# The output of a second feed-forward as seven block products in a phase of its own, on one Trainium2 core

## The chip, the cores and the metric

The kernel runs on one core of a Trainium2 chip. The metric is the device time of a run in microseconds (us), as the median of the runs; a profiled execution stands beside it, and all rows come from that. PE is TensorE (PEld its weight loads), DVE is VectorE, ACT is ScalarE, POOL is GpSimd, and SP is the engine whose queue issues nearly all DMAs.

## What is computed

Attention within chunks of 64 positions, then two feed-forward layers, all in float32:

```python
attn = softmax(q_c @ k_c.T / sqrt(64)); x = attn @ v_c      # x: 4608 x 512
h = x @ w_in; solu = h * softmax(h)                         # 1024 wide
x = ((solu - mean) / sqrt(var + 1e-6) * g_ln) @ w_out       # 4608 x 512
h = x @ w_in2; g = maximum(0.01 * h, h)                     # 2048 wide
out = g @ w_out2                                            # 4608 x 512
```

The weights arrive as float64 and are converted in the kernel by their bits. A float32 operand of a matmul is given as a high part, rounded to the matmul type float32r, and a low part, the rest. A product is then high x high, high x low and low x high: three matmuls.

## The kernel before

**The first phase** (L308 to L799) goes over 36 tiles t of 128 tokens: attention, first feed-forward with its softmax and normalisation, and its output y, which is stored by sixths (groups of 768 tokens) to `y_d` in DRAM. Beside this the weights are prepared in pieces. `load_next` loads a piece into one of four buffers, `take_magnitudes`, `convert_a` and `convert_b` convert it on ScalarE and VectorE, and `finish` calls the piece's `end`. `pieces` (L724) says how many an iteration takes: one, or two at t of 5 to 7. Of the 24 pieces, eight are of the first layer's w_out and sixteen of w_in2.

**The blocks.** The first product of the second layer, `h = y @ w_in2`, is computed by seven products of blocks in place of eight, in Winograd's form of Strassen's scheme. A piece of w_in2 for each half of the columns gives seven weight blocks (`want_in`, L172), split into high and low parts by ScalarE and GpSimd and stored to `wi_d` (L128). On the side of y, a group is cut into four blocks (a11, a21, a22, a12; two halves of 384 tokens, two halves of 512 features), four sums of them are made (`y_sum`), and seven operands are split (`y_split`): the high copy on ScalarE, the low part on GpSimd.

**The second phase** (L804 on) goes over 6 groups with 8 units j each. A unit is the seven products p1, p6, p2, p7, p5, p4, p3 in this order (`h2_product`), each of six matmuls of 384 columns, with weights that are streamed from `wi_d` by `w_load` into six buffers. The products use two PSUM banks in turn; p2 adds onto p1 in its bank, p7 onto p6, p4 onto that, p3 onto p5. What is read out between: p1 is copied by ScalarE, p6, p7, p5, p4 and p3 are added to kept results by VectorE (`with_ps`), and four of them end in `leaky`: Prelu on ScalarE, then high copy and low part (GpSimd) of an operand of the output product. So the bank of p4 must be read by VectorE before p1 of the next unit may write it (L825 to L828: the tags change sides with each unit).

The output product (`out_parts`) is a plain one: for each unit, twelve steps of six matmuls of 512 columns add to six PSUM banks, one per 128 tokens of the group. Two steps follow each of the first five products of the next unit, one each of the last two. Its weights w_out2 are converted once, in the first group, and stay in the core's memory (`wo_step`). Each engine runs its instructions in the order of the code, and DMAs on SP are issued in order; a DMA or instruction that waits holds up what is behind it on its queue.

## Time and profile before

| | |
|---|---|
| median of 3 runs | 1304.19 us (1303.96 to 1305.37) |
| the profiled execution | 1306.48 us, span 1304.7 us |
| granted TensorE clock, mean | 0.995 |
| busy share of the span: TensorE, weight loads, VectorE, ScalarE, GpSimd | 98%, 86%, 43%, 41%, 39% |
| DMA | 185.91 MB, mean 142 GB/s |

The span is the time from the first to the last instruction of the core; the execution's own time is 1.8 us longer. A busy time is a sum over instructions, so the engine with the largest share bounds the kernel only where it has no idle time between them. "Granted clock" is the share of 2.4 GHz that TensorE was given.

### The profile page before, as it was taken

How to read it: one execution, taken by the hardware profiler on the slowest of the kernel's cores; microseconds unless marked ns; L12 is line 12 of the kernel's file. 1: busy time of each engine (PE TensorE's matmuls, PEld its weight loads, DVE VectorE, ACT ScalarE, POOL GpSimd, SP SyncE). 2: the span in 40 equal slices, each digit the busy share in tenths (PEclk: the TensorE clock that was granted, in tenths of full speed). 3: DMA queues.
4: the chain of work that ended last, by engine and by line, in shares of the span. 5: the costliest groups of instructions: out<-in, count | busy, mean ns of one | idle time of the engine just before them, and what ended most of it. 6: DMA issues, size and time to landing. Idle time of an engine off the chain costs nothing.

```text
span 1304.7 us, 20560 instructions
## 1 busy us (share of the span) xinstructions
PE 1280.3 (98%) x7682; PEld 1118.3 (86%) x7682; DVE 556.6 (43%) x913; ACT 534.8 (41%) x1023; POOL 505.4 (39%) x601
## 2 busy tenths in 40 slices
PE   5999999999999999999999999999999999999998
PEld 4778888888888888889999999999999999999997
DVE  8678676767644443544641222122212221212112
ACT  6645445545443343344453334333333433343222
POOL 0356544555432222344572334234423532352222
PEclk9999999999999999999999999999999999999999
DMA  8435456554432214177654545544554455445342
GB/s 243 149 93 148 123 159 223 159 172 136 138 121 88 76 50 145 50 225 230 192 157 138 168 116 169 158 126 119 164 170 115 120 169 169 114 121 167 116 122 81
DMA packets 133778, 185.91 MB, mean 142 GB/s; under 512 B 47920, under 2 KB 69680, under 8 KB 132656
## 3 DMA queue, kind: packets, MB, share of 16 engines
q1 hardware_dynamic: 133232, 183.94, 47.0%
q8 instruction: 62, 1.02, 0.3%
q10 hardware_dynamic: 448, 0.66, 0.1%
q14 instruction: 36, 0.29, 0.1%
HBM read 151.00 MB, written 33.55 MB: 141 GB/s over the span
## 4 chain that ended last, share of the span: by engine, by line
PE 94%; DVE 2%; ACT 1%; DMA 1%; POOL 0%; issue 0%; SPq 0%; ACTq 0%
PE o_ps L877 30%; PE h_ps L834 27%; PE y_ps L505 15%; PE h_ps L423 14%; PE x_ps L395 3%; PE ln_ps L478 2%; PE s_ps L346 2%; PE pt_ps L379 1%; DMA raw<-in_w_in 1%; ACT es L577 0%; DMA qt<-in_q 0%; DVE wf L109 0%; DVE wf L105 0%; DVE wf L113 0%; DVE wf L103 0%
## 5 line engine op out<-in xcount | busy, mean ns | idle before, releaser
L877 PE MATMUL o_ps<-wo_s,g 128*128 128x512 f32 x1728 | 447.8, 391 | 0.8 <-POOL wo_s L303 0.8
L834 PE MATMUL h_ps<-yo,w_s 128*128 128x384 f32 x2016 | 406.9, 337 | 0.0
L834 PEld LDWEIGHTS h_ps<-yo,w_s 128*128 128x128 f32 x2016 | 362.8, 188 | 28.1
L816 POOL TENSOR_TENSOR g<-t,g 128x384 fp32r<-128x384 f32 x192 | 195.9, 1021 | 463.1 <-ACT g L815 389.9
L877 PEld LDWEIGHTS o_ps<-wo_s,g 128*128 128x128 f32 x1728 | 319.8, 188 | 43.0 <-POOL wo_s L303 1.3
L423 PE MATMUL h_ps<-wi,xs 128*128 128x512 f32 x864 | 211.5, 398 | 2.5 <-ACT xs L409 1.4
L505 PE MATMUL y_ps<-lnT,wo 128*128 128x512 f32 (+1 forms) x888 | 205.3, 387 | 1.0 <-POOL wo L120 0.8
L845 DVE TENSOR_TENSOR u<-h_ps,p 128x384 f32<-128x384 f32 x96 | 53.5, 557 | 335.1 <-PE h_ps L834 335.1
L423 PEld LDWEIGHTS h_ps<-wi,xs 128*128 128x128 f32 x864 | 160.2, 189 | 37.9 <-ACT xs L409 2.1
L505 PEld LDWEIGHTS y_ps<-lnT,wo 128*128 128x128 f32 x888 | 161.3, 188 | 34.7 <-DVE lnT L493 1.4
L813 ACT ACTIVATE t<-c 128x384 f32<-128x384 f32 x144 | 75.6, 525 | 264.6 <-DVE c L845 264.6
L369 POOL TENSOR_TENSOR es<-es,st 128x512 f32<-128x512 f32 x33 | 34.5, 1047 | 235.0 <-DVE st L368 211.0
L845 DVE TENSOR_TENSOR c<-h_ps,u 128x384 f32<-128x384 f32 x96 | 53.5, 557 | 129.4 <-PE h_ps L834 71.8
L815 ACT ACTIVATE g<-t 128x384 fp32r<-128x384 f32 x192 | 100.9, 526 | 6.1
L813 ACT ACTIVATE t<-h_ps 128x384 f32<-128x384 f32 x48 | 23.6, 491 | 186.1 <-PE h_ps L834 186.1
L445 DVE SCALAR_TENSOR_TENSOR us<-h_ps,us 128x1024 f32<-128x1024 f32 x36 | 44.1, 1225 | 61.3 <-ACT us L440 61.3
L440 ACT ACTIVATE us<-h_ps,z 128x1024 f32<-128x1024 f32 x36 | 40.1, 1115 | 54.7 <-DVE z L438 54.7
L513 ACT ACTIVATE ys<-y_ps 128x512 f32<-128x512 f32 x36 | 21.5, 596 | 99.8 <-PE y_ps L505 98.6
L493 DVE TENSOR_TENSOR lnT<-ln_ps,lnT 128x512 fp32r<-128x512 f32 x72 | 46.0, 681 | 33.7 <-ACT lnT L489 33.7
L413 DVE TENSOR_TENSOR xs<-x_ps,xs 128x512 fp32r<-128x512 f32 x36 | 24.8, 689 | 79.8 <-ACT xs L409 79.5
L845 DVE TENSOR_TENSOR c<-h_ps,p 128x384 f32<-128x384 f32 x48 | 26.8, 557 | 74.1 <-PE h_ps L834 74.1
L395 PEld LDWEIGHTS x_ps<-pt,vbd 128*64 128x64 f32 x1152 | 38.1, 142 | 15.7 <-issue 9.4
(87 smaller groups left out, 1153.5 us busy)
## 6 DMA issues: line engine op xcount, KB each, us to landing
w_s<-wi_d SPq DMA_DIRECT2D x336, 256.0 KB, 2.7
wi_d<-wi SPq DMA_DIRECT2D x8, 1792.0 KB, 7.6
raw<-in_w_out SPq DMA_DIRECT2D x24, 512.0 KB, 5.0
raw<-in_w_in SPq DMA_DIRECT2D x23, 512.0 KB, 4.4
vbd<-in_v SPq DMA_DIRECT2D x72, 128.0 KB, 3.6
a<-y_d SPq DMA_DIRECT2D x24, 384.0 KB, 5.7
qt<-in_q SPq DMA_DIRECT2D x35, 256.0 KB, 4.1
kbd<-in_k SPq DMA_DIRECT2D x70, 128.0 KB, 4.0
```

Source lines behind the costliest of these rows:

```text
L395: pe.matmul(ps[e * D : (e + 1) * D, i, c * D : (c + 1) * D], lhsT=vv[:, i, c, e], rhs=pp[:, i, c * D : (c + 1) * D], start=True, stop=True,)
L423: pe.matmul(h[:, n, :], lhsT=x[:, a, kk, :], rhs=w[:, b, kk % 2, n, :], start=(kk == 0 and a == 0 and b == 0), stop=(kk == KD - 1 and a == 1),
L440: act.activation(u, h, AF.Exp, bias=z[:, 0:1], accum_out=z[:, 1:2])
L445: dve.scalar_tensor_tensor(u, h, 1.0 / FF1, u, op0=ALU.mult, op1=ALU.mult, accum_out=z[:, 2:3])
L493: dve.tensor_tensor(dst[:, 1], ps, dst[:, 0].bitcast(F32), op=ALU.subtract)
L505: pe.matmul(ps[:, part], lhsT=w[:, a, kk % 4, m * P : (m + 1) * P], rhs=lnT[:, c, kk, pairs, :][:, part], start=(kk == 0 and a == 0 and c ...
L813: act.activation(t, src, AF.Prelu, alpha=0.01)
L815: act.activation(g[:, 0], t, AF.Copy)
L816: pool.tensor_tensor(g[:, 1], t, g[:, 0].bitcast(F32), op=ALU.subtract)
L834: pe.matmul(ps, lhsT=w[:, a, kk * P : (kk + 1) * P], rhs=y[:, c, kk, :], start=(first and kk == 0 and a == 0 and c == 0), stop=(kk == 1 an ...
L845: dve.tensor_tensor(o, ps, x, op=ALU.add)
L877: pe.matmul(ps, lhsT=x[:, a, i * P : (i + 1) * P], rhs=wos[j][:, h, c, :], start=(j == 0 and h == 0 and a == 0 and c == 0), stop=(j == QUA ...
```

## The change

The output product is computed by the same seven-product scheme. For a group, all eight units of the first product now run one after the other, and their results stay as four blocks (c11, c21, c22, c12), each in four tiles of two units (`leaky`, `blocks`). Sums of blocks (`block_sum`) are made on VectorE, three of them a pair of units, after products p6, p2 and p7 of units 2, 4 and 6; operands (`block_split`) by ScalarE and VectorE, the first four after p5 of units 1, 3, 5 and 7. Then come 28 slots of output (seven products of four pairs), each of six times a matmul of 512 columns (the high part against high and low weights, side by side) and one of 256 (the low part against the high weights), into two PSUM tiles of three banks. A slot's weights, 512 KB, are streamed from `wo_d` into six buffers (`wo_load`). Results are added on VectorE (`result`) and stored a product later (`out_store`).

w_out2's blocks are prepared in the first phase as those of w_in2 are (`want_out2`), so it has 40 pieces and sixteen stores; six more iterations take two pieces (`DOUBLE`), and the store of a block is issued at the start of an iteration. All low parts of operands in the second phase are on VectorE; nine tiles of w_in2 are loaded ahead instead of six. The last product of the last group goes token tile by token tile, so that its results leave early.

```diff
+PAIRS = QUADS // 2
+SLOTS = 7 * PAIRS
...
-WS = 6
+WS = 9
+WOS = 6
+RING = 11
 
 AHEAD = 5
+DOUBLE = (5, 6, 7, 10, 14, 18, 22, 26, 30)
...
+    wo_d = [dram.tile([P, 7, 2, 2, 2 * P], F32, name=f"wo_d{i}") for i in range(PAIRS)]
...
+    def want_blocks(srcs, dst):
...
-            stores.append((wi_d[j], w.bitcast(F32)))
-
+            stores.append((dst, w.bitcast(F32)))
+
+        for src in srcs:
+            queue.append((src, KD * P, end))
+
+    def want_in(j):
+        srcs = []
         for h in range(2):
             i, c = divmod((j + QUADS * h) * P, 512)
-            src = w_in2[i].rearrange("p (k n) -> p k n", k=KD)[:, :, c : c + P]
-            queue.append((src, KD * P, end))
+            srcs.append(w_in2[i].rearrange("p (k n) -> p k n", k=KD)[:, :, c : c + P])
+        want_blocks(srcs, wi_d[j])
+
+    def want_out2(j):
+        i, a = divmod(j, 4)
+        rows = w_out2.rearrange("(h i) p f -> i p h f", h=2)[i]
+        srcs = [rows[:, :, a * DM + c : a * DM + c + 2 * P] for c in (0, 2 * P)]
+        want_blocks(srcs, wo_d[j // 2][:, :, j % 2])
...
-    def y_load(g):
+    def y_load(g, n):
         if g < NG:
...
+            name, r, c = (("a11", 0, 0), ("a21", 1, 0), ("a22", 1, 1), ("a12", 0, 1))[n]
+            yr[name] = yp.tile([P, 2, TH], F32, tag=name, name=name)
+            sync.dma_start(
+                out=yr[name], in_=y_d[g][:, 2 * c : 2 * c + 2, r * TH : (r + 1) * TH]
+            )
...
-                "s2": ("s1", "a11", ALU.subtract, None),
                 "s3": ("a11", "a21", ALU.subtract, "a21"),
+                "s2": ("s1", "a11", ALU.subtract, "a11"),
...
+    def operand(x):
+
+        o = yp.tile([P, 2, 2, TH], F32R, tag="ring", bufs=RING, name="yo")
+        act.activation(o[:, 0], x, AF.Copy)
+        dve.tensor_tensor(o[:, 1], x, o[:, 0].bitcast(F32), op=ALU.subtract)
+        return o
+
     def y_split(g, k):
         if g < NG:
             x = yr[("a11", "s2", "a12", "s3", "s1", "a22", "s4")[k]]
-            o = yo[g, PRODUCTS[k]] = yp.tile([P, 2, 2, TH], F32R, tag="yo", bufs=9, name="yo")
-            act.activation(o[:, 0], x, AF.Copy)
-            for i in range(2):
-                eng = dve if g == 0 and i == 0 else pool
-                eng.tensor_tensor(o[:, 1, i], x[:, i], o[:, 0, i].bitcast(F32), op=ALU.subtract)
-
...
+    wo_tiles = []
+    wo_order = ((i, name) for _ in range(NG) for name in PRODUCTS for i in range(PAIRS))
+
+    def wo_load():
+        at = next(wo_order, None)
+        if at:
+            w = wb.tile([P, 2, 2, 2 * P], F32R, tag="wo", bufs=WOS, name="wo_s")
+            sync.dma_start(out=w.bitcast(F32), in_=wo_d[at[0]][:, w_place[at[1]]])
+            wo_tiles.append(w)
...
-                    store_next()
...
+            for j in range(QUADS):
+                want_out2(j)
...
+                    for n in range(4):
+                        y_load(0, n)
...
+                store_next()
...
-                pieces = 0 if t in (1, 4) or t >= T - 2 else 2 if AHEAD <= t < AHEAD + 3 else 1
+                pieces = 0 if t in (1, 4) or t >= T - 2 else 2 if t in DOUBLE else 1
...
+                    y_split(0, 0)
+                    for name in ("s1", "s3", "s2"):
+                        y_sum(0, name)
+                    y_split(0, 1)
+                    y_sum(0, "s4")
+                    for k in range(2, 7):
+                        y_split(0, k)
...
 
-            t = wb.tile([P, TH], F32, tag="t", name="t")
-            act.activation(t, src, AF.Prelu, alpha=0.01)
-            g = gts[n, block] = wb.tile([P, 2, TH], F32R, tag="g", bufs=8, name="g")
-            act.activation(g[:, 0], t, AF.Copy)
-            pool.tensor_tensor(g[:, 1], t, g[:, 0].bitcast(F32), op=ALU.subtract)
+            j = n % QUADS
+            if j % 2 == 0:
+                blocks[block, j // 2] = wb.tile(
+                    [P, 2, TH], F32, tag=f"{block}{j // 2}", name=f"{block}{j // 2}"
+                )
+            act.activation(blocks[block, j // 2][:, j % 2], src, AF.Prelu, alpha=0.01)
...
+        def block_sum(name, i):
+            x, y, op, to = {
+                "s1": ("c21", "c22", ALU.add, None),
+                "s3": ("c11", "c21", ALU.subtract, "c21"),
+                "s2": ("s1", "c11", ALU.subtract, "c11"),
+                "s4": ("c12", "s2", ALU.subtract, "c12"),
+            }[name]
+            if to:
+                blocks[name, i] = blocks[to, i]
+            else:
+                blocks[name, i] = wb.tile([P, 2, TH], F32, tag=f"{name}{i}", name=f"{name}{i}")
+            dve.tensor_tensor(blocks[name, i], blocks[x, i], blocks[y, i], op=op)
+
+        operands = {}
+
+        def block_split(s):
+            p, i = divmod(s, PAIRS)
+            x = blocks[("c11", "s2", "c12", "s3", "s1", "c22", "s4")[p], i]
+            operands[s] = operand(x)
+
+        sums = {}
+
+        def out_matmuls(p, i, kk, m, whole=True):
+            x, w = operands[p * PAIRS + i], wo_now[i]
+            ps = sums[p % 2][:, m]
+            first = p in (0, 1, 4) and i == 0 and kk == 0
+            last = i == PAIRS - 1 and kk == 1
+            c = slice(m * P, (m + 1) * P)
+            if whole:
+                pe.matmul(
+                    ps,
+                    lhsT=x[:, 0, kk, c],
+                    rhs=w[:, kk].rearrange("p a n -> p (a n)"),
+                    start=first,
+                    stop=False,
+                    skip_group_check=True,
+                )
+            else:
+                for a in range(2):
+                    pe.matmul(
+                        ps[:, : 2 * P],
+                        lhsT=x[:, 0, kk, c],
+                        rhs=w[:, kk, a],
+                        start=False,
+                        stop=False,
+                        skip_group_check=True,
+                    )
+            pe.matmul(
+                ps[:, : 2 * P],
+                lhsT=x[:, 1, kk, c],
+                rhs=w[:, kk, 0],
+                start=False,
+                stop=last,
+                skip_group_check=True,
+            )
+
+        wo_now, results = {}, {}
+
+        def out_product(s):
+            p, i = divmod(s, PAIRS)
+            if i == 0 and p in (0, 1, 4):
+                sums[p % 2] = pso.tile([P, 3, 512], F32, tag=f"o{p % 2}", name="o_ps")
+            wo_now[i] = wo_tiles.pop(0)
+            wo_load()
+            for kk in range(2):
+                for m in range(3):
+                    out_matmuls(p, i, kk, m)
+
+        def plus(o, p, a, x, m=slice(0, 3)):
+            dve.tensor_tensor(o[:, m], sums[p % 2][:, m, a * 2 * P : (a + 1) * 2 * P], x[:, m], op=ALU.add)
+
+        def result(p, m=slice(0, 3), halves=(1, 0)):
+
+            name = PRODUCTS[p]
+            if name in ("p1", "p6", "p2", "p7") and m.start == 0:
+                tag = {"p1": "p1", "p6": "u2", "p2": "c", "p7": "u3"}[name]
+                results[tag] = wb.tile([P, 3, 2 * P], F32, tag=f"o_{tag}", name=f"o_{tag}")
+            to, x = {
+                "p1": ("p1", None),
+                "p6": ("u2", "p1"),
+                "p2": ("c", None),
+                "p7": ("u3", "p1"),
+                "p5": ("u3", "u3"),
+                "p4": ("p1", "p1"),
+                "p3": ("u2", "u2"),
+            }[name]
+            o = results[to]
+            for a in halves:
+                if x is None:
+                    act.activation(o[:, m], sums[p % 2][:, m, 2 * P :], AF.Copy)
+                else:
+                    plus(o, p, a, results[x], m)
+                x = to
+
+        def out_store(g, p, eng=sync, m=slice(0, 3), rows=slice(0, P)):
+            at = {"p2": ("c", 0, 0), "p5": ("u3", 1, 1), "p4": ("p1", 1, 0), "p3": ("u2", 0, 1)}
+            if PRODUCTS[p] not in at:
+                return
+            o, r, c = at[PRODUCTS[p]]
+            first = g * TILES + 3 * r
+            dst = out[first : first + 3].rearrange("t p n -> p t n")
+            eng.dma_start(
+                out=dst[rows, m, c * 2 * P : (c + 1) * 2 * P], in_=results[o][rows, m]
+            )
+
+        for g in range(NG):
+            for j in range(QUADS):
+                if g == 0 and j < WOS:
+                    wo_load()
+                elif g and j == 1:
+                    out_store(g - 1, 6)
+                elif g and 2 <= j < 6:
+                    y_load(g + 1, j - 2)
+                for k in range(7):
+                    h2_product(g * QUADS + j, k)
+                    if g and j == 7 and k < 2:
+                        y_sum(g + 1, ("s1", "s3")[k])
+                    if j % 2 == 1 and k == 4:
+                        block_split(j // 2)
+                    if j % 2 == 0 and j and 1 <= k < 4:
+                        block_sum(("s1", "s3", "s2")[k - 1], j // 2 - 1)
+            for s in range(SLOTS):
+                p, i = divmod(s, PAIRS)
+                tail = g == NG - 1 and p == 6
+                if tail:
+                    wo_now[i] = wo_tiles.pop(0)
+                else:
+                    out_product(s)
+                if s < 2:
+                    for name in ("s1", "s3") if s == 0 else ("s2",):
+                        block_sum(name, PAIRS - 1)
+                if s + PAIRS < SLOTS:
+                    block_split(s + PAIRS)
+                if 9 <= s < 9 + PAIRS:
+                    block_sum("s4", s - 9)
+                for at, name in ((15, "s1"), (17, "s3")):
+                    if g == 0 and s == at:
+                        y_sum(g + 1, name)
+                if 19 <= s < 26:
+                    if s == 20:
+                        y_sum(g + 1, "s2")
+                    elif s == 23:
+                        y_sum(g + 1, "s4")
+                    y_split(g + 1, s - 19)
+                if g == 0 and s in (2, 5, 8, 11):
+                    y_load(1, s // 3)
+                if p and i == PAIRS - 1:
+                    out_store(g, p - 1)
+                if i == PAIRS - 1 and not tail:
+                    result(p)
+                    if g == NG - 1 and p == 4:
+                        plus(results["u2"], p, 1, results["u2"], slice(2, 3))
+        for m in range(3):
+            for i in range(PAIRS):
+                for kk in range(2):
+                    out_matmuls(6, i, kk, m, whole=m < 2)
+            if m:
+                result(6, slice(m - 1, m))
+                out_store(NG - 1, 6, sync, slice(m - 1, m))
+        result(6, slice(2, 3), (0,))
+        for eng, rows in ((sync, slice(0, 64)), (act, slice(64, P))):
+            out_store(NG - 1, 6, eng, slice(2, 3), rows)
```

## Rows read from the trace of the kernel before

**Rows 1.** The page, section 1: engine, busy us, share, instructions

```profile
PE 1280.3 (98%) x7682; PEld 1118.3 (86%) x7682; DVE 556.6 (43%) x913; ACT 534.8 (41%) x1023; POOL 505.4 (39%) x601
```

**Rows 2.** Windows, one group: us, busy of each engine, granted clock, DMA share, GB/s

```profile
676.40:801.00 124.60, 124.60 (x626) 112.99 (x625) 28.98 (x48) 42.94 (x82) 47.05 (x48) 1.00 0.49 144
```

**Rows 3.** The chain in order of time, two stretches: start us, us, what

```profile
528.76 0.70 DVE lnT L493
...
529.50 22.36 PE y_ps L505 x120
...
686.02 1.37 PE o_ps L877 x6
687.39 1.05 PE h_ps L834 x6
...
701.60 1.37 PE o_ps L877 x6
```

**Rows 4.** Timeline of the first unit: start us, us, engine, line, operation

```profile
551.71 8.53 PE L834 MATMUL h_ps<-yo,w_s 128*128 128x384 f32 x48
...
557.15 0.56 DVE L845 TENSOR_TENSOR c<-h_ps,u 128x384 f32<-128x384 f32 x1 [0.49 <-PE h_ps L834]
557.74 0.52 ACT L813 ACTIVATE t<-c 128x384 f32<-128x384 f32 x1 [1.13 <-DVE c L845]
```

**Rows 5.** Lines by form: busy us, mean ns of one, idle before and releaser

```profile
L813 ACT ACTIVATE t<-c 128x384 f32<-128x384 f32 x144 | 75.6, 525 | 264.6 <-DVE c L845 264.6
L845 DVE TENSOR_TENSOR c<-h_ps,u 128x384 f32<-128x384 f32 x96 | 53.5, 557 | 129.4 <-PE h_ps L834 71.8 <-ACT g L815 57.6
...
L255 ACT ACTIVATE yo<-a 128x768 fp32r<-128x768 f32 x24 | 19.9, 834 | 0.0
```

**Rows 6.** Timeline of VectorE at the third group's additions

```profile
747.18 1.41 DVE L249 TENSOR_TENSOR s<-a,a 128x768 f32<-128x768 f32 x1
750.87 0.56 DVE L845 TENSOR_TENSOR u<-h_ps,p 128x384 f32<-128x384 f32 x1 [2.28 <-PE h_ps L834]
751.34 0.95 DVE L249 TENSOR_TENSOR s<-s,a 128x768 f32<-128x768 f32 x1
```

**Rows 7.** Timeline of ScalarE in the first phase, two instructions in a row

```profile
168.71 0.67 ACT L96 ACTIVATE wf<-raw 128x512 f32<-128x512 f32 x1
169.28 0.59 ACT L385 ACTIVATE pt<-pt_ps 128x512 f32<-128x512 f32 x1
```

**Rows 8.** Windows of 3 us while the first weights are loaded

```profile
517.00:520.00 3.00, 3.00 (x15) 2.48 (x14) 1.73 (x2) 1.20 (x2) 1.52 (x3) 1.00 1.02 400
```

**Rows 9.** Windows, four iterations with pieces of weights and four without

```profile
151.52:209.30 57.78, 57.78 (x434) 47.83 (x433) 40.94 (x64) 28.53 (x50) 29.45 (x40) 1.00 0.54 174
382.46:440.08 57.62, 57.62 (x434) 47.90 (x433) 26.37 (x44) 22.93 (x40) 14.73 (x28) 1.00 0.25 74
```

**Rows 10.** Timeline of VectorE, low part of x, after one piece

```profile
176.35 0.69 DVE L413 TENSOR_TENSOR xs<-x_ps,xs 128x512 fp32r<-128x512 f32 x1 [2.26 <-ACT xs L409]
```

**Rows 11.** The page, section 5: the output's matmuls

```profile
L877 PE MATMUL o_ps<-wo_s,g 128*128 128x512 f32 x1728 | 447.8, 391 | 0.8 <-POOL wo_s L303 0.8
```

**Rows 12.** Timeline of the end

```profile
1291.74 9.00 PE L877 MATMUL o_ps<-wo_s,g 128*128 128x512 f32 x39
...
1301.42 0.42 DVE L888 COPY o<-o_ps 128x256 f32<-128x256 f32 x1 [1.31 <-ACT o L887]
```

**Rows 13.** Windows of 2 us in the first phase

```profile
72.00:74.00 2.00, 0.00 (x0) 0.00 (x0) 1.97 (x3) 1.88 (x4) 0.00 (x0) 1.00 0.94 314
74.00:76.00 2.00, 1.88 (x34) 1.88 (x36) 1.08 (x5) 1.93 (x5) 0.69 (x1) 0.53 0.62 205
76.00:78.00 2.00, 2.00 (x19) 1.70 (x18) 1.13 (x2) 1.35 (x3) 1.64 (x6) 0.61 0.18 42
```

**Rows 14.** Windows of 4 us near the start

```profile
12.00:16.00 4.00, 2.66 (x27) 2.21 (x25) 3.50 (x8) 3.40 (x19) 0.00 (x0) 1.00 1.11 308
```

**Rows 15.** Timeline of TensorE in that window

```profile
14.80 1.09 PE L346 MATMUL s_ps<-kbd,qt 128*64 128x128 f32 x16 [1.23 <-DMA kbd<-in_k]
```

More of the change, by code (lines that the diff above doesn't have):

```diff
@@ L170, in want_out1 @@
             queue.append((src, 4 * P, end))
-    def want_in(j):
+    def want_blocks(srcs, dst):
         kept = []
@@ L253, in y_split @@
             x = yr[("a11", "s2", "a12", "s3", "s1", "a22", "s4")[k]]
-            o = yo[g, PRODUCTS[k]] = yp.tile([P, 2, 2, TH], F32R, tag="yo", bufs=9, name="yo")
-            act.activation(o[:, 0], x, AF.Copy)
-            for i in range(2):
-                eng = dve if g == 0 and i == 0 else pool
-                eng.tensor_tensor(o[:, 1, i], x[:, i], o[:, 0, i].bitcast(F32), op=ALU.subtract)
-    Y_STEPS = [
-        ((4, 0), lambda g: y_split(g, 0)),
-        ((5, 0), lambda g: y_sum(g, "s1")),
-        ((5, 2), lambda g: y_sum(g, "s2")),
-        ((5, 4), lambda g: y_sum(g, "s3")),
-        ((6, 0), lambda g: y_split(g, 1)),
-        ((6, 3), lambda g: y_sum(g, "s4")),
-    ] + [((7, k - 1), lambda g, k=k: y_split(g, k)) for k in range(2, 7)]
+            yo[g, PRODUCTS[k]] = operand(x)
     w_tiles = []
@@ L700 @@
                     )
-                    y_load(0)
-                    stage = ctx.enter_context(
-                        tc.tile_pool(name="st2", bufs=2, side="right", reuse_waits="tile")
-                    )
-                    wf_bufs = 2
+                    for n in range(4):
+                        y_load(0, n)
                     for _ in range(WS):
                         w_load()
-                    for h in range(2):
-                        wo_load(0, h)
                 if t <= AHEAD:
@@ L899 @@
-        NQ = NG * QUADS
-        for n in range(NQ + 1):
-            g, j = divmod(n, QUADS)
-            parts = out_parts(n - 1) if n else iter(())
-            if n == NQ:
-                for _ in parts:
-                    pass
-                break
-            if j == 3:
-                y_load(g + 1)
-            for k in range(7):
-                h2_product(n, k)
-                for _ in range(2 if k < 5 else 1):
-                    next(parts, None)
-                if n == 0 and 2 <= k < 4:
-                    wo_load(1, k - 2)
-                if g == 0 and k < 6:
-                    for h in range(2):
-                        if (3 if j == 0 else 0) <= k - h < 5:
-                            wo_step(j, h, k - h)
-                for at, do in Y_STEPS:
-                    if at == (j, k):
-                        do(g + 1)
+        def block_sum(name, i):
[10 more added lines that the diff above has]
+            dve.tensor_tensor(blocks[name, i], blocks[x, i], blocks[y, i], op=op)
```

79 lines of the change are left out of this document (5 added, 74 removed).

## The prediction

> **What bounds the kernel now.** I read the page's busy times first, then the windows of one group of the second feed-forward, the chain of waits, and the timelines at the places that the change touches. TensorE is busy 98% of the span [rows 1], and in a group it is busy all of 124.60 us at full clock, with VectorE at 29, ScalarE at 43 and GpSimd at 47 [rows 2]. There only the columns and the count of its matmuls set the time. The chain gives the price of both [rows 3]: six matmuls of 384 columns take 1.05 us, six of 512 take 1.37. More exactly, a unit (seven products of six matmuls and 36 of the output) lasts 701.60 - 686.02 = 15.58 us; with 0.2288 for 512 columns, 384 take (15.58 - 36 x 0.2288) / 42 = 0.1749. For 256 columns: the stretch of 120 took 22.36 us, 72 of them of 512 (16.47), which leaves 5.89 for 48, 0.1227 each, each with a weight load of its own.
>
> **The products.** Before, a group's output is 48 steps of 6 matmuls of 512: 288 x 0.2288 = 65.88 us. After, 28 slots of six pairs, 512 and 256 columns: 168 x (0.2288 + 0.1227) = 59.04. That is 6.84 less a group, 41.0 over six. The rows have these two shapes apart; that their alternation costs nothing is my choice, since 384 and 512 alternate without a loss [rows 3].
>
> **What the interleaving hid.** This step decides. Before, each product is followed by one or two output steps, so where two steps follow the products come 1.05 + 1.37 = 2.42 us apart. Afterwards they stand alone, 1.05 us apart, on the same two PSUM banks (L825 to L828). A bank is read by ScalarE or VectorE before the product after next may write it. The one place in the trace where products stand alone already is the first unit [rows 4]: with VectorE otherwise idle, p5's addition starts 0.19 us after the product's last issue (551.71 + 5.25 = 556.96 to 557.15) and takes 0.557 [rows 5]; TensorE follows a VectorE end by 0.04 (528.76 + 0.70 to 529.50, [rows 3]), ScalarE by 0.03 [rows 4]. That is 0.79 of 1.05 us: it fits, with 0.26 to spare. One more VectorE instruction of 768 elements, 0.95 us [rows 6], doesn't, and the change puts such instructions there. Two independent instructions in a row overlap by 0.09 on VectorE (750.87 + 0.557 against 751.34, [rows 6]) and by 0.10 on ScalarE [rows 7].
>
> Odd units (an operand is split after p5), in us from the unit's first matmul: p5 ends at 5.25; its addition 5.44 to 6.00; Prelu on ScalarE 6.03 to 6.55 (0.525, [rows 5]); behind it the operand's high copy, 6.45 to 7.29 (0.834); VectorE waits for that, low part 7.32 to 8.27; queued behind it is p4's addition, 8.18 to 8.74. The next unit's p1 writes p4's bank and starts at 8.78 instead of 7.35: a wait of 1.43.
>
> Even units (three block sums after p6, p2, p7): p6 ends at 2.10; its addition 2.29 to 2.85; then without a hole two sums, p7's addition and the third sum, to 5.90; p5's addition 5.81 to 6.37. p3 needs that bank at 6.30 and starts at 6.41: a wait of 0.11.
>
> Unit 0 has no such work, and after unit 7 the output writes other banks. So three waits of each kind a group, 18 of each in all: 25.7 + 2.0 = 27.7 us. Bounds: nothing, if the copy were made before VectorE comes to it (p4's addition would then end at 7.33); with no overlap and a low part of 1.41, which 747.18 took beside GpSimd [rows 6], 2.16 and 0.59, 50 in all. I take 0.95 for the low part, since GpSimd has nothing left to do after the first phase.
>
> The Trainium skill, page "SBUF — State Buffer", section "SBUF: two separate sides", says that a VectorE instruction with two SBUF inputs and a GpSimd instruction that reads SBUF lock each other out for its whole length. The trace agrees, 1.41 against 0.95; were GpSimd still at work beside the splits, the odd waits would be 18 x 0.46 = 8 us longer.
>
> **The output phase.** VectorE has 24 splits there, 7 of the next group, 7 block sums, up to 4 group sums and 12 results, 54 x 0.95 = 51 of 59 us; ScalarE 33 x 0.83 = 27. Operands are made four slots (8.4 us) ahead. The worst product is the sixth: 12 instructions, 11.4 us in 8.4, so 3 late where 8.4 are to spare. A result has a product's 8.4 us until its bank is written again. I take no wait. If the cover went, each late operand would show at once, up to 3 us a group, 18 in all.
>
> **Loads and queues.** All this stands on SP in order: a group's 56 loads of 256 KB, 28 of 512 KB, four of y, now one by one, and four stores, 32.5 MB in some 122 us, 265 GB/s. Now it is 144 GB/s at a DMA share of 0.49 [rows 2], 294 scaled to a full share; three microseconds with the same kinds of loads moved 400 GB/s [rows 8]. Nine tiles ahead are eight products, 8.4 us; a store waits for VectorE, but is queued a product after its result. Taken at nothing.
>
> **The first phase.** It takes over w_out2: sixteen more pieces, eight more blocks stored. Four iterations with four pieces and two blocks take 57.78 us, four without 57.62, TensorE full in both [rows 9]; the difference on VectorE is 14.57, so 3.6 a piece. New are iterations with two pieces that also end a block: VectorE 6.6 + 7.3 = 13.9 of 14.4 us. It now idles 2.26 before the low part of x [rows 10], which takes most of the second piece; the rest, 1.4, would be late six times: bounds 0 and 8, and I take 0.5, since TensorE needs that low part only an iteration later. The block's store moves on SP ahead of the piece loads, the stores of y and the three loads of q and k; it waits there for GpSimd, and what is behind it is needed an iteration later. The conversion in the first group goes, with TensorE's 0.8 us for its weights [rows 11].
>
> **The end.** The last matmul is through at 1291.74 + 9.00 = 1300.74, 3.96 before the span's end; VectorE's last half ended at 1301.84, 2.86 before it [rows 12]. Afterwards 0.2 + 0.42 + 2.86 = 3.5, so 0.5 less; eight matmuls cut in two add 8 x 0.0166 = 0.1.
>
> **Sum.** -41.0 + 27.7 + 0.5 - 0.8 - 0.5 + 0.1 = -14.0 on a span of 1304.7 (1306.48 the profiled execution). The runs' median lies 2.3 below that, 1304.19; the same 14 from it is 1290. A measurement of this kernel tells 0.2%, 2.6 us, from no change.
>
> **Rivals.**
> 1. *The waits are mostly not there*, because the copies are made early: 27.7 becomes 0 to 14, 1262 to 1276. For: p4's addition fits if the copy comes a microsecond sooner. Against: ScalarE has the copy behind a Prelu that waits for VectorE. 0.12.
> 2. *The waits eat the gain.* Without the overlap the odd wait is 1.70 and the even 0.59: 18 x 2.29 = 41.2, and 1304. That the change does nothing lies here. For: an instruction that waits for another engine may lose the overlap. Against: the overlap stands in the rows. 0.10.
> 3. *The clock falls at the waits, and it is slower.* After 2.27 us without a matmul the granted clock was 0.53 and 0.61 in two windows of 2 us [rows 13], 1.2 GHz for most of them: 0.94 + 0.78 = 1.7 us lost. At each odd wait, 18 x 1.7 = 31, less the 2 of the even waits, which slower products hide: 1319. It turns the change into a loss from 9 falls of the 18. Against: in 12 to 16 us, with an idle of 1.23 [rows 14, 15], the clock stayed at 1.00, and my 1.43 stand alone in 17 us. 0.13.
> 4. *The stream of weights falls behind*: 195 MB at 250 GB/s are 780 us instead of 749: 1335; slower than before under 261 GB/s. Against: rows 8. 0.05.
>
> The Trainium skill, page "TensorE: Matmul & The Clock Gate", section "A second HAM failure mode: psum-queue depth-cycling", tells of a kernel that cycles through PSUM banks and whose clock went back and forth over the short idles between groups of matmuls. By that rule rival 3 comes true, 1319; no row here shows it for an idle as short.
>
> **How the numbers follow.** The forecast has 0.60 and a range of its own of 1282 to 1299 (odd wait 1.0 to 1.8, front 0 to 3). The range for 8 in 10, 1276 to 1310, takes in the forecast, rival 2 and the near edges of 1 and 3. Faster: 0.60 + 0.12 + half of rival 2 = 0.78 with the edges; same 0.07; slower 0.15.
>
> **What would show it.** Right: a group of some 122.5 us, 63.4 for the products and 59 for the output; TensorE idle some 1.4 us at the end of units 1, 3 and 5, put down to VectorE's addition after p4, with a ScalarE copy before it; no idle in the output's slots; the first product of the second feed-forward at about 552. Wrong: no such holes (rival 1), 2.3 a pair (2), a granted clock under 1.00 after 552 (3), TensorE waiting for DMA (4), or a first phase that ends after 556.

## The result and the profile after

The changed kernel takes 1313.93 us (median of 4 runs, 1312.27 to 1316.21) against 1304.11 of the kernel before beside it: a ratio of 1.0074, 95% interval 1.0057 to 1.0092. It is slower by 0.7%, and above the range that was forecast. The profiled execution took 1316.21 us, its span is 1314.4.

Section 1 of the page of after (engine, busy us, share, instructions), which answers to [rows 1]: TensorE is busy 20.6 us less, VectorE 58% more.

```profile
PE 1259.7 (96%) x7978; PEld 1104.6 (84%) x7978; DVE 879.8 (67%) x1280; ACT 567.9 (43%) x1006; POOL 270.5 (21%) x356
```

Windows of after, the products of the first group, its output, and the products of the second (columns as in [rows 2]):

```profile
563.05:627.83 64.78, 60.80 (x338) 58.25 (x337) 31.05 (x50) 22.34 (x43) 0.00 (x0) 1.00 0.83 270
627.83:687.17 59.34, 59.34 (x338) 51.54 (x337) 48.12 (x55) 25.79 (x35) 0.00 (x0) 1.00 0.88 284
687.17:752.03 64.86, 60.88 (x339) 58.32 (x338) 34.71 (x55) 21.75 (x42) 0.00 (x0) 1.00 0.84 267
```

A group takes 64.78 + 59.34 = 124.1 us, 122.5 were forecast, 124.60 it took before. The granted clock is 1.00 in all three. And the first product stands at 563.05, not at 551.71 as in [rows 4].

TensorE's timeline of after in the iteration t = 13 of the first phase, where before there was no idle. It is a late iteration (`late` in the kernel: every fourth, t = 5, 9, 13 and so on), in which the products for y come behind the attention's product and not ahead of it:

```profile
195.96 0.60 PE L373 MATMUL pt_ps<-ident,es 128*128 128x128 f32 x4
196.39 1.04 PE L472 MATMUL ln_ps<-ident,us 128*128 128x128 f32 x8
199.67 1.89 PE L389 MATMUL x_ps<-pt,vbd 128*64 128x64 f32 x32 [2.24 <-ACT pt L379]
201.33 1.93 PE L340 MATMUL s_ps<-kbd,qt 128*64 128x128 f32 x16
```

VectorE, and then ScalarE, at the same place:

```profile
193.90 1.41 DVE L191 TENSOR_TENSOR wc<-wf,wc 128x256 f32<-128x256 f32 x1
195.35 0.84 DVE L192 TENSOR_TENSOR wc<-wf,wc 128x256 f32<-128x256 f32 x1
196.11 1.21 DVE L432 TENSOR_REDUCE z<-h_ps 128x1 f32<-128x1024 f32 x1
```

```profile
196.28 1.06 ACT L194 ACTIVATE wi<-wc 128x1024 fp32r<-128x1024 f32 x1 [2.31 <-DVE wc L192]
197.36 1.11 ACT L434 ACTIVATE us<-h_ps,z 128x1024 f32<-128x1024 f32 x1
198.46 0.66 ACT L101 ACTIVATE wf<-raw 128x512 f32<-128x512 f32 x1
199.03 0.59 ACT L379 ACTIVATE pt<-pt_ps 128x512 f32<-128x512 f32 x1
```

To read from below: the attention's product (L389) waits for ScalarE's copy of `pt`; that stands behind a step of a piece (L101) and the exponential (L434). The exponential waits for VectorE's reduction (L432), which is queued behind two sums of a weight block (L191, L192; `wc`) that ended there. It stands behind ScalarE's copy of those sums, too (L194, which waits for L192). The reduction ends at 197.32 and that copy at 197.34, so the trace doesn't tell which of the two held it; both lead back to the sums. The other thirteen blocks end at other iterations, and there is no such idle at any of them. The same idle, 2.23 us, comes back at 318.91 (t = 21) and 438.31 (t = 29). Those three iterations last 18.3 us, as against 14.6 before. That is 3.7 each, of which the idle is 2.2. The rest stands in the windows behind it (after; the last three columns are the granted clock, DMA share and GB/s):

```profile
199.00:201.00 2.00, 1.33 (x26) 1.33 (x28) 1.93 (x6) 2.00 (x5) 0.78 (x1) 0.70 0.27 115
201.00:203.00 2.00, 2.00 (x28) 1.86 (x24) 1.93 (x3) 1.22 (x3) 1.81 (x3) 0.50 1.09 459
203.00:205.00 2.00, 2.00 (x12) 1.50 (x9) 1.97 (x5) 0.00 (x0) 1.70 (x5) 0.94 0.86 344
```

In the second phase, TensorE (two of the 18 like these), ScalarE and VectorE at the end of unit 1, and VectorE in unit 2, all of after:

```profile
579.14 15.41 PE L824 MATMUL h_ps<-yo,w_s 128*128 128x384 f32 x84 [1.32 <-DVE h_c L835]
595.88 15.41 PE L824 MATMUL h_ps<-yo,w_s 128*128 128x384 f32 x84 [1.32 <-DVE h_c L835]
```

```profile
576.37 0.53 ACT L806 ACTIVATE c<-h_c 128x384 f32<-128x384 f32 x1 [2.18 <-DVE h_c L835]
576.80 0.83 ACT L270 ACTIVATE yo<-c 128x768 fp32r<-128x768 f32 x1
```

```profile
577.66 0.96 DVE L271 TENSOR_TENSOR yo<-c,yo 128x768 fp32r<-128x768 f32 x1 [1.33 <-ACT yo L270]
578.54 0.55 DVE L835 TENSOR_TENSOR h_c<-h_ps,h_p 128x384 f32<-128x384 f32 x1
...
581.63 0.56 DVE L835 TENSOR_TENSOR h_u<-h_ps,h_p 128x384 f32<-128x384 f32 x1 [2.07 <-PE h_ps L824]
582.10 0.95 DVE L865 TENSOR_TENSOR s<-c,c 128x768 f32<-128x768 f32 x1
583.09 0.96 DVE L865 TENSOR_TENSOR c<-c,c 128x768 f32<-128x768 f32 x1
583.96 0.55 DVE L835 TENSOR_TENSOR h_u<-h_ps,h_p 128x384 f32<-128x384 f32 x1
584.43 0.95 DVE L865 TENSOR_TENSOR c<-s,c 128x768 f32<-128x768 f32 x1
585.29 0.55 DVE L835 TENSOR_TENSOR h_c<-h_ps,h_u 128x384 f32<-128x384 f32 x1
```

The odd wait is there as forecast, link by link: copy 0.83, low part 0.96, p4's addition 0.55 at 578.54, the next product 0.05 after it. But two units take 595.88 - 579.14 = 16.74 us, and fourteen products of 1.05 are 14.7; one idle of 1.32 is not the whole of 2.05. The group of the products (page, section 5) shows the same: 18 idles are 23.8 us, and the busy column, too, is above 2016 x 0.1749 = 352.6.

```profile
L824 PE MATMUL h_ps<-yo,w_s 128*128 128x384 f32 x2016 | 366.3, 339 | 23.9 <-DVE h_c L835 23.8
```

The end, TensorE and then VectorE (after), which answers to [rows 12]: a wait of 0.98 ahead of the last token tile; its last matmul is through at 1309.8, 4.6 before the span's end.

```profile
1306.70 0.50 PE L893 MATMUL o_ps<-wo_s,yo 128*128 128x256 f32 x2 [0.98 <-DVE o_u L923]
```

```profile
1309.84 1.22 DVE L923 TENSOR_TENSOR o_u<-o_ps,o_u 128x256 f32<-128x256 f32 x3 [3.19 <-PE o_ps L901]
```

### The profile page after: what moved, and what is told of

Read it like the earlier page. It is cut to its first block, busy times and chain, and to the rows that moved or that the text cites. A ratio compares the mean times of both kernels' runs of the same rounds, so it can differ in the third digit from the quotient of the medians.

```text
span 1314.4 us, 21334 instructions
## 1 busy us (share of the span) xinstructions
PE 1259.7 (96%) x7978; PEld 1104.6 (84%) x7978; DVE 879.8 (67%) x1280; ACT 567.9 (43%) x1006; POOL 270.5 (21%) x356
## 3 DMA queue, kind: packets, MB, share of 16 engines
q8 instruction: 64, 1.05, 0.3%
## 4 chain that ended last, share of the span: by engine, by line
PE 84%; DVE 6%; ACT 4%; issue 2%; POOL 1%; DMA 1%; ACTq 0%; SPq 0%; DVEq 0%; POOLq 0%
PE h_ps L824 25%; PE o_ps L883 18%; PE y_ps L499 13%; PE h_ps L417 11%; PE o_ps L901 9%; PE x_ps L389 3%; PE s_ps L340 2%; PE ln_ps L472 2%; DVE h_c L835 2%; DMA kbd<-in_k 1%; ACT yo L270 1%; PE pt_ps L373 1%; DVE lnT L487 1%; ACT c L806 1%; DVE es L353 1%
## 5 line engine op out<-in xcount | busy, mean ns | idle before, releaser
L824 PE MATMUL h_ps<-yo,w_s 128*128 128x384 f32 x2016 | 366.3, 339 | 23.9 <-DVE h_c L835 23.8
L883 PE MATMUL o_ps<-wo_s,yo 128*128 128x512 f32 x1000 | 353.5, 397 | 0.0
L901 PE MATMUL o_ps<-wo_s,yo 128*128 128x256 f32 x1008 | 283.7, 281 | 0.0
L883 PEld LDWEIGHTS o_ps<-wo_s,yo 128*128 128x128 f32 x1000 | 187.7, 188 | 46.2
L901 PEld LDWEIGHTS o_ps<-wo_s,yo 128*128 128x128 f32 x1008 | 190.0, 188 | 0.0
L271 DVE TENSOR_TENSOR yo<-c,yo 128x768 fp32r<-128x768 f32 x144 | 132.5, 952 | 31.9 <-ACT yo L270 31.9
L806 ACT ACTIVATE c<-h_c 128x384 f32<-128x384 f32 x144 | 74.2, 525 | 176.7 <-DVE h_c L835 174.7
L835 DVE TENSOR_TENSOR h_u<-h_ps,h_p 128x384 f32<-128x384 f32 x96 | 53.4, 556 | 124.6 <-PE h_ps L824 124.6
L270 ACT ACTIVATE yo<-c 128x768 fp32r<-128x768 f32 x144 | 113.1, 839 | 8.4 <-DVE c L865 6.8
L439 DVE SCALAR_TENSOR_TENSOR us<-h_ps,us 128x1024 f32<-128x1024 f32 x36 | 44.1, 1224 | 58.8 <-ACT us L434 58.8
L835 DVE TENSOR_TENSOR h_c<-h_ps,h_u 128x384 f32<-128x384 f32 x96 | 53.2, 554 | 33.4 <-PE h_ps L824 30.1
L270 ACT ACTIVATE yo<-a 128x768 fp32r<-128x768 f32 x36 | 30.0, 842 | 72.8 <-DVE a L265 72.8
L389 PEld LDWEIGHTS x_ps<-pt,vbd 128*64 128x64 f32 x1152 | 39.1, 145 | 22.2 <-ACT pt L379 12.4
```

The costliest lines, as they stand in the source:

```text
L270: act.activation(o[:, 0], x, AF.Copy)
L271: dve.tensor_tensor(o[:, 1], x, o[:, 0].bitcast(F32), op=ALU.subtract)
L389: pe.matmul(ps[e * D : (e + 1) * D, i, c * D : (c + 1) * D], lhsT=vv[:, i, c, e], rhs=pp[:, i, c * D : (c + 1) * D], start=True, stop=True,)
L439: dve.scalar_tensor_tensor(u, h, 1.0 / FF1, u, op0=ALU.mult, op1=ALU.mult, accum_out=z[:, 2:3])
L806: act.activation(blocks[block, j // 2][:, j % 2], src, AF.Prelu, alpha=0.01)
L824: pe.matmul(ps, lhsT=w[:, a, kk * P : (kk + 1) * P], rhs=y[:, c, kk, :], start=(first and kk == 0 and a == 0 and c == 0), stop=(kk == 1 an ...
```

## The experiments

Theory: the forecast gain is there, and three things take it: idles in the first phase where a block's sums stand in VectorE's queue just ahead of a late iteration (11 us), the odd waits, and the even waits at more than was forecast (37 us together). Rivals: the sixteen more pieces cost the first phase their time wherever they stand; the addition is late through ScalarE's or PSUM's own work; the weights come late.

**1. Other iterations with two pieces** (changed kernel otherwise).

```diff
-DOUBLE = (5, 6, 7, 10, 14, 18, 22, 26, 30)
+DOUBLE = (5, 6, 7, 10, 11, 18, 19, 26, 27)
```

> Same 40 pieces and 16 blocks of weights, but two pieces are taken at t of 10, 11, 18, 19, 26 and 27 instead of 10, 14, 18, 22, 26 and 30, so that no block of weights ends in the iteration just ahead of a late one (after the change it did at t of 12, 20 and 28). Theory: the first phase is longer because a block that ends there holds up ScalarE's exponential, hence its copy of the attention weights, and TensorE stands idle 2.2 us and then runs at the lower clock for a while: 3 x 3.7 us. Expected: the first phase ends at 552 to 553 us instead of 563, the three idles are gone, the time is 1303 us. Rival (the sheer load of sixteen more pieces makes the phase longer): it ends at 560 or later, 1311 to 1316 us.

Measured: 1307.86 us (1306.78 to 1309.12), ratio to before 1.0024 (1.0014 to 1.0033), 5 us above what the theory had. The first product of the second phase stands at 555.58, between the theory's 553 and the rival's 560. No block ends ahead of the late iterations now, and yet an idle is left at the same three (1.23 to 1.25 us). TensorE at t = 13, and the windows:

```profile
198.19 1.15 PE L389 MATMUL x_ps<-pt,vbd 128*64 128x64 f32 x32 [1.23 <-ACT pt L379]
```

```profile
197.00:201.00 4.00, 2.81 (x52) 2.50 (x53) 3.73 (x8) 3.73 (x9) 1.28 (x2) 1.00 0.29 64
201.00:205.00 4.00, 4.00 (x19) 3.08 (x18) 3.93 (x7) 0.00 (x0) 3.66 (x6) 1.00 0.25 68
```

The iteration takes 15.9 in place of 18.3. The idle is shorter by 1.0, and the clock stays at 1.00: the matmuls behind it took 1.15 in place of 1.89. What keeps the 1.23 is by the trace VectorE coming late out of two double iterations in a row; that was not tried by itself.

**2. The odd waits alone**: the high copy two products earlier, the low part in the next unit.

```diff
-                    if j % 2 == 1 and k == 4:
-                        block_split(j // 2)
+                    if j % 2 == 1 and k == 2:
+                        operands[j // 2] = high_part(blocks["c11", j // 2])
+                    if j % 2 == 0 and j and k == 0:
+                        low_part(operands[j // 2 - 1], blocks["c11", j // 2 - 1])
...
+                if s == 0:
+                    low_part(operands[3], blocks["c11", 3])
```

(`high_part` and `low_part` are the two halves of `operand`; unit 7 has no next unit, so its low part follows the first slot of the output.)

> One part is moved: the operand of c11 gets its high copy on ScalarE right after p2's Prelu of the odd unit, and its low part on VectorE in the next even unit after p1, where VectorE is idle. Same instructions, same counts. Theory (p4's addition is queued on VectorE behind a low part that waits for a ScalarE copy): the odd wait of 1.40 us and the 0.13 us of starting again go, 18 x 1.53 = 27.5 us less, the three block sums of an even unit keep costing 0.5: a pair of units takes 15.2 us instead of 16.74, time 1286 us. Rival (the streamed weights come late at the units' ends): 1314, the waits stay. Rival (VectorE has too much to do in these units): 1310 or more, the wait moves to another product.

Measured: 1284.62 (1282.17 to 1285.14), ratio 0.9844 (0.9829 to 0.9858), the products of a group 60.05. This one move makes the change a gain. The products' row of the page:

```profile
L830 PE MATMUL h_ps<-yo,w_s 128*128 128x384 f32 x2016 | 361.3, 338 | 0.2
```

No idle is left, and the busy column fell too, by 5.0: the odd waits cost 23.7 + 5.0 = 28.7, or 1.59 each.

**3. The even waits alone**: the three block sums in three gaps of two units.

```diff
-                    if j % 2 == 0 and j and 1 <= k < 4:
-                        block_sum(("s1", "s3", "s2")[k - 1], j // 2 - 1)
+                    for dj, kk, name in ((0, 0, "s1"), (0, 1, "s3"), (1, 1, "s2")):
+                        if j >= 2 and j % 2 == dj and k == kk:
+                            block_sum(name, j // 2 - 1)
```

(The group sums s1 and s3 go from unit 7 into the output in all groups.)

> One part is moved: of the three block sums of a pair of units, two follow p1 and p6 of the even unit and the third follows p6 of the odd unit, instead of all three between p6 and p5 of the even one; the two sums for the next group go to the output phase in all groups, as they are in the first. Theory: the even wait (0.5 of a pair's 2.05 us) goes and the odd one stays: a pair takes 16.2 us, 18 x 0.5 = 9 us less, 1305 us. Rival (weights late): no change, 1314.

Measured: 1306.29 (1303.14 to 1307.18), ratio 1.0010 (1.0001 to 1.0019), the products 63.38 a group.

```profile
L824 PE MATMUL h_ps<-yo,w_s 128*128 128x384 f32 x2016 | 357.4, 336 | 23.8 <-DVE h_c L835 23.8
```

The idle is as in after, and 8.9 us went out of the busy column alone. So the even waits cost 8.9, 0.49 each, and none of it shows as idle.

**4. All three together.** The list of 1, the moves of 2, and the sums of 3, with s1 a product later and s3 after p1 of the odd unit.

> The three edits together: blocks end elsewhere in the first phase, high copy after p2 and low part in the next unit after p1, one block sum at a time where VectorE is idle (after p6 of the even unit, after p1 and p6 of the odd one). Theory: the first phase ends at 552 to 553, products of a group take 58.9 us instead of 64.85, TensorE idles nowhere in the second phase before its last product: 1313.9 - 11 - 36 = 1267 us, 2.9% faster than the kernel before. If only parts of the theory hold: 1275 to 1300.

Measured: 1270.55 (1270.48 to 1272.19), ratio 0.9743 (0.9728 to 0.9757). The products take 58.5 us a group without any idle, the output 59.34; the 1.25 us idles of run 1 remain, and with them the 3.5 that it is above the expectation.

**5. Another engine at the same place**: the low part of the changed kernel's early operands on GpSimd.

```diff
-                        block_split(j // 2)
+                        operands[j // 2] = high_part(blocks["c11", j // 2])
+                        low_part(operands[j // 2], blocks["c11", j // 2], pool)
```

> Nothing is moved in time; only the engine of the low part of the first four operands of a group (made after p5 of units 1, 3, 5, 7) changes from VectorE to GpSimd. Theory (p4's addition is late because it is queued on VectorE behind a low part that itself waits for ScalarE's copy): the 18 idles of 1.40 us at the end of odd units go, the products of a group take 60.0 us in place of 64.8 as when the low part was moved a unit later, and the time is 1285. Rival (the addition is late by ScalarE's work or by the read of PSUM itself): the idles stay and the time is 1314. Rival by the lock of the two engines (a GpSimd instruction beside the addition stretches it): the addition of 0.56 us takes up to 1 us more and some 0.5 us of each idle stays: 1294.

Measured: 1284.88 (1284.46 to 1287.32), ratio 0.9852 (0.9838 to 0.9867), the products 60.09: as run 2. GpSimd, and VectorE beside it (the additions of p4 and p3):

```profile
577.47 1.86 POOL L273 TENSOR_TENSOR yo<-c,yo 128x768 fp32r<-128x768 f32 x1 [42.24 <-ACT yo L269]
```

```profile
576.57 0.56 DVE L841 TENSOR_TENSOR h_c<-h_ps,h_p 128x384 f32<-128x384 f32 x1 [0.48 <-PE h_ps L830]
577.68 0.56 DVE L841 TENSOR_TENSOR h_c<-h_ps,h_u 128x384 f32<-128x384 f32 x1 [0.55 <-PE h_ps L830]
```

The low part takes twice as long there, and nobody waits for it. p4's addition now waits for its product alone and is done before the low part starts. So it was late by its place in VectorE's queue, behind a low part that waited for ScalarE's copy; the addition itself needs neither, and the read of PSUM is no longer than before: p3's addition, beside GpSimd's low part, takes 0.56 as ever.

**6. The block's conversion an iteration later**, with the moves of run 4 and the changed kernel's own list.

```diff
-                    finish(pieces)
+                    if t < 8 or t % 4:
+                        finish()
...
-                        finish(pieces)
+                        finish()
```

> The three moved steps of the second phase as in the run that joined them, but the first phase keeps the changed kernel's own list of iterations with two pieces; only the block's conversion (high copy on ScalarE, sums on VectorE) that fell into the iteration just ahead of those at 13, 21 and 29 is made one iteration later, behind the first feed-forward's matmuls. Theory (the 2.24 us idles at 13, 21 and 29 come from that conversion, and the clock's fall after them doubles their price): no idle before the attention's product there, no window under a granted clock of 1.00, first phase ends at 552 to 553, time 1260 to 1263 where the second phase is 707, at most 1266. Rival (the idles come from the sixteen more pieces as such, wherever they stand): they move by one iteration, the first phase ends at 556 to 563, time 1270 to 1274.

Measured: 1266.40 (1266.03 to 1266.88), ratio 0.9707 (0.9692 to 0.9721), with run 11 the fastest of all, and 3% faster than before. The three iterations take 14.65, the first product stands at 550.89. (The expected 1260 to 1263 had left out the end: 550.89 and six groups of 117.9 make 1258.3, the span's end is at 1264.2.) Windows of the first group, and the products' row of the page:

```profile
550.89:609.43 58.54, 58.54 (x337) 58.54 (x336) 32.14 (x51) 22.88 (x44) 0.00 (x0) 1.00 0.89 299
609.43:668.78 59.35, 59.35 (x338) 51.55 (x337) 47.54 (x54) 25.59 (x35) 0.00 (x0) 1.00 0.88 284
```

```profile
L831 PE MATMUL h_ps<-yo,w_s 128*128 128x384 f32 x2016 | 352.3, 335 | 0.0
```

**7. The same edit of the first phase alone, in the changed kernel.**

> The changed kernel with one edit alone: a block's conversion that falls into the iteration ahead of those at 13, 21 and 29 is made an iteration later; the second phase keeps its waits. Theory (the 11.3 us by which the first phase ends late are these three idles and the clock's fall behind them): first phase ends at 551.5 to 552.5, no idle before the attention's product at 13, 21, 29, time 1314 - 11 = 1303, no difference from the kernel before. Rival (VectorE's and ScalarE's sixteen more pieces cost the time wherever they stand): 556 to 563, 1307 to 1314.

Measured: 1304.37 (1303.15 to 1306.81, 11 runs), ratio 0.9998 (0.9988 to 1.0007): level with before. The three idles are gone, the iterations take 14.65. The first product stands at 554.08, 9.0 sooner than in after; this profile is 2.1 us later than that of after already ahead of the first of the three iterations, which makes 11.1 for the three. By the medians it is 9.6. The edit moves a block's sums on VectorE and its copies on ScalarE together, so it doesn't tell their parts in the delay apart.

**8. TensorE kept busy in the idle** (changed kernel; the result of the added transposes is not used).

```diff
+            def fill(n):
+                s = bank("s", "fill")
+                for _ in range(n):
+                    pe.transpose(s[:, :P], ident, ident)
...
             def attend(t):
-
+                if t in (13, 21, 29):
+                    fill(16)
                 pv_mm(t + 1)
```

> The changed kernel with sixteen transposes of the identity (128x128, their result read by nobody) put on TensorE ahead of the attention's product at 13, 21 and 29, where it idles 2.24 us; the wait for ScalarE's copy stays as long. Theory (of the 3.7 us that each of these iterations lost, some 1.5 are the clock's fall to 0.50 to 0.70 after the idle): the granted clock stays at 1.00 there, each iteration takes 16.7 in place of 18.3, the time falls by 4 to 5 us to 1309.5. Rival (the matmuls behind the idle are slow for another reason, as VectorE's and ScalarE's lateness): iterations of 18.3 and 1314.

Measured: 1310.45 (1309.72 to 1310.80), ratio 1.0044 (1.0031 to 1.0057), iterations of 16.84. TensorE at t = 13, and windows:

```profile
196.76 1.91 PE L520 MATMUL fill<-ident 128*128 128x128 f32 x16
199.16 1.15 PE L389 MATMUL x_ps<-pt,vbd 128*64 128x64 f32 x32 [0.49 <-ACT pt L379]
```

```profile
199.00:201.00 2.00, 1.84 (x48) 1.79 (x48) 1.90 (x7) 2.00 (x5) 0.78 (x2) 1.00 0.54 229
201.00:203.00 2.00, 2.00 (x12) 1.58 (x9) 1.93 (x3) 0.69 (x3) 1.72 (x5) 1.00 1.08 452
```

The copy comes no sooner: from the transposes ahead to the attention's product it is 199.16 - 195.45 = 3.71 us, as in after (199.67 - 195.96). The clock stays at 1.00 at all three, and each iteration is 1.45 us shorter: that is the clock's part of the 3.7. Two traces show the same price without the transposes. Runs 2 and 3 have the changed kernel's first phase and its three idles, but at t = 13 the clock did not fall, and the iteration took 16.86 and 16.85; at 21 and 29 it fell, and they took 18.30 to 18.32. Run 2 at t = 13:

```profile
198.19 1.15 PE L395 MATMUL x_ps<-pt,vbd 128*64 128x64 f32 x32 [2.22 <-ACT pt L385]
```

```profile
198.00:200.00 2.00, 1.80 (x48) 1.79 (x48) 1.90 (x7) 2.00 (x4) 0.77 (x2) 1.00 0.54 229
```

So the fall is not certain: it came after ten of the twelve such idles in after and in runs 2, 3 and 5. That the transposes prevent it rests on three idles of three.

**9. Less prefetch** in the version of run 6: `WS` 6 for 9, `WOS` 4 for 6. **10.** `WS` 6 alone.

> As the run with the block's conversion one iteration later, with six tiles of the first product's weights loaded ahead in place of nine, and four of the output's in place of six. Theory (the loads keep ahead of TensorE by a wide margin; the deeper prefetch is worth nothing): same time within 0.2%, no idle of TensorE put down to a DMA in the second phase. Rival (the stores and loads of y that wait on the queue use up the margin): idles of 0.5 to 3 us at the start of a group's products or of its output, 12 places, 6 to 30 us longer.

> The version with all edits that helped so far, with six tiles of the first product's weights loaded ahead in place of nine, and the output's six kept. Theory (six tiles are 6.3 us of products ahead, less than the 6.5 us that a load took at most; nine are 9.4): the products of a group take 60.0 to 61.5 us in place of 58.5 as when both depths were cut, idles of 0.3 to 1.5 us before a product are put down to a DMA, the output stays at 59.34, time 1266 + 6 x 2.1 = 1279. Rival (it was the output's four tiles that drained the queue for both): products at 58.5, time 1266 to 1268.

Measured: 1287.58 (1284.99 to 1289.47) and 1280.97 (1280.39 to 1284.86). The theory of run 9 fell. TensorE's waits of run 9 (us in total, times, longest), and two windows of its first products:

```profile
PE h_ps L831 <- DMA w_s<-wi_d: 7.9, 9, 1.5
PE o_ps L890 <- DMA wo_s<-wo_d: 4.7, 5, 2.5
```

```profile
564.00:568.00 4.00, 2.55 (x15) 2.25 (x14) 1.67 (x3) 1.86 (x3) 0.00 (x0) 1.00 0.98 331
580.00:584.00 4.00, 3.10 (x18) 2.81 (x17) 1.95 (x4) 2.15 (x4) 0.00 (x0) 1.00 0.99 362
```

In run 10 the output is back at 59.34 and the products are not (60.3 to 62.4), as expected. So the depth of the first product's weights is worth 14.6 us, and that of the output's, with six of the first, 6.6 more. The tile's view of run 6, issue to landing of a 256 KB load (us):

```profile
DMA to landing us min/median/max: 2.8/4.0/6.6
```

Six buffers give a load five products, 5 x 1.05 = 5.2 us; nine give eight, 8.4. The longest load lies between. Whether the changed kernel, which is slower itself, would have felt the smaller depth was not tried.

**11. The order of the shapes** in the output (run 6's version): three matmuls of 512 columns in a row, then three of 256.

> As the run with the block's conversion one iteration later, but in the output each three matmuls of 512 columns come in a row and then the three of 256, in place of one of each in turn. Theory (alternating the two shapes costs 59.34 - 59.04 = 0.30 us a group): the output phase takes 59.04 and the time falls by 1.8 us. Rival (the 0.30 belongs to the switch of a slot or to the weight load of each matmul, which stay): 59.3 and the same time.

Measured: 1266.40 (1265.92 to 1268.09), the output 59.34 as before. The theory fell: the alternation costs nothing. Where 0.30 us a group come from stays open; my 0.1227 for 256 columns was what was left of a stretch, and (59.34 - 168 x 0.2288) / 168 is 0.1244.

## Why the prediction was wrong

The span was forecast at 1304.7 - 14.0 = 1290.7 and is 1314.4, 23.7 more. By its steps:

- **The products** (-41.0): right. Without waits the products take 58.5 us a group (58.8 forecast) and the output 59.34 (59.04). The two nearly cancel. (The 0.2288 for 512 columns that both forecasts rest on is finer than the rows have it: 1.37 for six is 0.2283.)
- **The first phase** (+0.5) is the step that failed: it ends 11.3 us later. With that loss taken back the change is level with before (run 7), so it is what makes a loss of it; the waits below took the gain. I had counted VectorE's time in an iteration, 13.9 of 14.4 us, and given what would be late an iteration's grace. But VectorE's work need not be late for its own consumer: the sums of a block stand in its queue ahead of the reduction (and their copy in ScalarE's ahead of the exponential), two steps from the copy that TensorE waits for, and in a late iteration only 1.0 us of transposes covers that copy, where the others have 5.7 us of products for y. I priced a full engine by its load where its order decided. Run 7 takes the step back and run 8 splits its price: 2.2 of idle and 1.5 of clock, three times, 11.1. In the kernel before, the blocks ended at other iterations, so its windows [rows 9] could not show it. But those of [rows 13], which I read for the clock alone, have a wait of the same make: the reduction queued behind the conversion of a piece, ScalarE's exponential and copy late by it, and the attention's product waiting. VectorE, then TensorE (before):

```profile
69.78 0.69 DVE L113 SCALAR_TENSOR_TENSOR wf<-raw,wf 128x512 uint32<-128x512 uint32 x1
70.39 1.22 DVE L438 TENSOR_REDUCE z<-h_ps 128x1 f32<-128x1024 f32 x1
```

```profile
74.12 1.98 PE L395 MATMUL x_ps<-pt,vbd 128*64 128x64 f32 x32 [2.28 <-ACT pt L385]
```

- **The odd waits** (25.7): mechanism right and size nearly, 28.7 measured (1.59 each: 1.32 of idle, the rest in the busy column).
- **The even waits** (2.0): mis-sized, 8.9. After the idle the unit's p6 was read at 581.63, 0.20 later from the unit's first matmul than I had it (579.14 + 2.29). The two sums did not overlap as [rows 6] have it: the second starts 0.04 after the first's end (582.10 + 0.95 to 583.09) and not 0.09 ahead of it. It writes the tile c21, which the first reads; that this is the reason was not tried. So p5's addition ends at 585.84, and p3, due 6.30 after the unit's start, at 585.44, waits 0.45 in place of 0.11. In sum the waits are 37.6. That is near the 41.2 of rival 2, which by the prediction's own links are 39.2 (1.62 and 0.56 without the overlap, not 1.70 and 0.59). Its reason, the lost overlap, is there at the even waits alone: at the odd ones the copy starts 0.10 before Prelu's end and p4's addition 0.08 before the low part's.
- **The output phase, loads and queues** (nothing): right. No idle in the output before the last tile and no wait for a DMA at 267 to 284 GB/s, so rival 4 is not there. In run 6's version that hangs on the depth of the prefetch (runs 9 and 10).
- **The end** (-0.5): +1.6, since TensorE waits 0.98 for VectorE's read ahead of the last token tile, and the last store lands 1.1 later than I had taken.
- **Rival 3** gave the nearest time, 1319, for a reason that is not there: behind idles of 1.32 us, eighteen of them, the granted clock is 1.00 throughout the products. That it came nearest is luck. The clock did fall, at 2.24 us, in the first phase, where I had not looked for an idle. What the Trainium skill, page "TensorE: Matmul & The Clock Gate", section "A second HAM failure mode: psum-queue depth-cycling", tells of another kernel does not carry over to the idles between these products: the trace has 1.00 there.

So 10.8 (first phase) + 9.9 (waits) + 2.1 (end) + 1.8 (output) - 1.6 (products) = 23.0 of the 23.7.

The Trainium skill, page "SBUF — State Buffer", section "SBUF: two separate sides", has VectorE and GpSimd block each other where VectorE's instruction has two SBUF inputs or runs in a 2-port perf mode. Run 5 agrees: beside GpSimd's 1.86 us the addition, with one input in PSUM, took 0.56 as before.

## What to carry to other kernels

Where work is added to an engine that isn't full, don't ask how full it is but what is queued behind each added instruction and how much work covers that at this very place; iterations of a pipeline that look alike can have 5 us of cover or 1. Products that are moved into a phase of their own lose the work that hid the reads of their banks: before the gain in columns counts, each read between two products must fit into the time of one, behind a wait too, where the first read came 0.20 us later. Deepen the prefetch until the load that lands slowest, not the median one, fits into the products that cover it.

## What was not expected of the hardware

After idles of 2.24 us TensorE's granted clock was 0.70 and 0.50 in two windows, 1.2 GHz for most of them (1.45 us more each by run 8), while idles of 1.23 to 1.32 us left it at 1.00. But the same idle need not cost it: after idles of 2.22 to 2.24 us at t = 13, 21 and 29 it fell in ten cases of twelve. And ahead of the attention's product between 72 and 75 us, where all thirteen traces have an idle of 2.26 to 2.30 us, it fell in six. Part of a wait stands in the busy column: 14.0 of the 37.6 us of waits were in the products' busy time (366.3 against 352.3 without waits), so a short wait is read from the distance between starts, not from idle. Some of it is in how the rows are drawn: such a matmul lasts 0.33 us and the next one starts 0.175 after it, so an idle behind it is 0.16 shorter than the delay. And the DMAs moved 299 GB/s for 58 us without an idle of TensorE (run 6), though with six tiles ahead TensorE waited in windows in which they moved 331 and 362.
